# The even w_gate chunks of an attention and SwiGLU kernel: two tiles become one, with the four row blocks of a chunk in another place and another order

## The chip, the core and the metric

The kernel runs on one core of a Trainium2 chip. The metric is the device time of one execution in microseconds (us); the time before is the median of three runs.

## The reference, cut to what matters

Batch 8, 8 heads, 576 positions, 64 elements per head, all in float32. The attention output is laid out as 4608 rows of 512 and goes through a gated feed-forward layer.

```python
scores = (1.0 / np.sqrt(64)) * np.matmul(q, k.transpose(0, 1, 3, 2))
scores = np.where(block_i >= block_j, scores, -1e9)      # blocks of 64 positions
attn = softmax(scores)                                   # rows
x = np.matmul(attn, v).transpose(0, 2, 1, 3).reshape(4608, 512)
g = x @ w_gate                                           # 512 x 1536
silu = g * (1.0 / (1.0 + np.exp(-g)))
out = (silu * (x @ w_val)) @ w_out                       # 1536 x 512
```

## The kernel before

Attention runs by batch and by pairs of heads: TensorE makes scores, VectorE and GpSimd the maxima, ScalarE the exponentials, TensorE the products with v. The feed-forward layer runs on 18 tiles of 256 rows of x. Every float32 operand of its products is split into a high and a low part (`float32r`), and a product is the sum of three matmuls: high by high, high by low, low by high.

In `feed_forward`, each of the 18 tiles walks through the 12 column chunks of 128 of w_gate and w_val two at a time. For one such pair, `up(i, 0)` multiplies x with w_gate's even chunk and then with its odd chunk, and `up(i, 1)` does the same with w_val. A chunk has four blocks of 128 rows (d = 0 to 3, the four blocks of x^T in `xhl`), each with three matmuls of 256 columns: 12 matmuls a chunk, with the weights as the stationary operand (lines 1109 to 1111). The down products with w_out have the activations `hhl` as the stationary operand and 512 columns (lines 1201 to 1203).

All of w_gate and w_val stays in SBUF. `g_odd0`, `g_odd1` (high and low part of the odd chunks), `v_all0`, `v_all1` (w_val) and `g_even0`, `g_even1` are tiles of the pool `const`, placed one after the other. A tile `gap` of 64 bytes stands ahead of `g_even0`. In the built program `g_odd` starts at bytes 1984 and 14272 of a partition and `v_all` at 26560 and 51136, which is 192 modulo 256; `g_even` starts at 75776 and 88064, which is 0 modulo 256. The steps between a tile's blocks and chunks are multiples of 512 bytes, so each block of 128 columns starts at the same byte modulo 256 as its tile.

`weight(i, kind)` brings a chunk from HBM, puts its two int32 words together (ScalarE and VectorE) and writes the high part with ScalarE and the low part with VectorE into the place that `w_at` names. For six chunks, w_out's parts wait in such a place too (`AWAY`), before that place gets its own weights.

The order of all engines comes from a planner in the kernel, `in_order()`. Each piece of work is a task with an engine, a cost and a rank, and each waits for named others. In tiles 0 to 3 (`j < FINE`) the up product of each d is a task of its own, which waits for that d's x; from tile 4 on, the 12 matmuls of a chunk are one task. The x of tile 0 comes from the heads in turn: d = 0 from heads 0 and 1, d = 3 from heads 6 and 7. Where the plan leaves TensorE idle for over 0.3 us, `keep_busy` writes small matmuls of a tile of ones (line 1418) into the order ahead of the next task. After the first 8 us of the plan it writes `int(FILL * t.gap / 0.107)` of them, with `FILL` 0.6. Nothing reads their output. A change of what a task waits for can so move every later task, on every engine.

Of the kernel before, what the change touches and what calls it, by code (L numbers as in the profile page):

```python
# [7 lines left out]
F32 = mybir.dt.float32  # L8
F32R = mybir.dt.float32r
# [9 lines left out]
def kernel(  # L19
# [17 lines left out]
    nc = tc.nc  # L37
# [3 lines left out]
    P = 128  # L41
# [5 lines left out]
    NDC = DM // P  # L47
    NFC = DFF // P
# [12 lines left out]
    FINE = 4  # L61
# [35 lines left out]
    const = ctx.enter_context(tc.tile_pool(name="const", bufs=1))  # L97
# [55 lines left out]
    def add(engine, cost, rank, fn, after=(), bufs=(), port=False, mode="", stage=""):  # L153


        t = Task(engine, cost, rank, fn, after, bufs, port, mode)
        for a in after:
            if a is not None:
                a.next.append(t)
                t.waits += 1  # L160
        for u in bufs:
            u.left += 1
        t.n, t.stage = len(tasks), stage
        tasks.append(t)
        return t


    def act_us(n, psum=False, more=0.0):
        return (0.05 if psum else 0.093) + n * 0.000833 + more

    def dve_us(n, one=False):
        return 0.07 + n * (0.00052 if one else 0.00104)

    def up_us(n):
        return n * 0.1134 + (0.012 if n < 3 * NDC else 0.0)
# [8 lines left out]
    def dma(rank, size, fn, after=(), bufs=(), n=1, engine="SP", packet=1024, late=0.0):  # L184

        t = add(engine, 0.5 * n, rank, fn, after, bufs)
        t.moves = size / packet * (6.0 + 0.0485 * packet) / 16e3
        t.late = 1.1 + late
        return t
# [12 lines left out]
    half_w, whole_w = [P, NDC, DFF // 2], [P, NDC, DFF]  # L202
    g_odd = [const.tile(half_w, F32R, name=f"g_odd{x}") for x in range(2)]
    v_all = [const.tile(whole_w, F32R, name=f"v_all{x}") for x in range(2)]
    const.tile([P, 16], F32, name="gap")
    g_even = [const.tile(half_w, F32R, name=f"g_even{x}") for x in range(2)]

    def w_at(which, x, i):

        if which:  # L210
            return v_all[x][:, :, i * P : (i + 1) * P]
        return (g_odd if i % 2 else g_even)[x][:, :, i // 2 * P : (i // 2 + 1) * P]

# [98 lines left out]
    for i in range(7):  # L314
        n = 2**i
# [594 lines left out]
    def words(ap):  # L910
        return ap.bitcast(I32) if wide else ap
# [11 lines left out]
    def weight(i, kind):  # L923

        R = PIECES[i][kind]
        raw = Buf("wo", "raw")
        away = AWAY.get(i) if kind == 2 else None
        wo = Buf("wo", "out") if kind == 2 and not away else None
        fs = slice(i * P, (i + 1) * P)

        parts = 1 if wo else NDC

        def part(j):  # L940
            if wo:
                return wo[0][:, j : j + 1]
            which, c = away or (kind, i)
            return w_at(which, j, c)

        def load():
            view = raw[0].rearrange("p (n m) -> p n m", n=NDC if kind < 2 else 1)
            if kind < 2:
                fs = slice(i * P * (1 + wide), (i + 1) * P * (1 + wide))
                src = words((w_gate, w_val)[kind])[:, fs].rearrange("(c p) f -> p c f", p=P)  # L950
            else:
                src = words(w_out)[i * P : (i + 1) * P, :].rearrange("p (n m) -> p n m", n=1)
            nc.sync.dma_start(out=view, in_=src)

        t = chain["w"] = dma(AHEAD.get((i, kind), R), 5e5, load, [chain["w"]], [raw], packet=1024 if kind < 2 else 4096)
        bufs = [raw, wo] if wo else [raw]

        def words_of(j):
            w = raw[0].rearrange("p (n t) -> p n t", t=1 + wide)[:, :, j]
            return w.rearrange("p (n m) -> p n m", n=parts)  # L960

        y = Buf("ob", "signs") if wide else None


        def signs():
            w = words_of(1).bitcast(F32)
            to = y[0].rearrange("p (n m) t -> p n m t", n=parts)[:, :, :, 1]
            nc.scalar.mul(to, w, 2.0**-60)

        def scaled():  # L970
            w = words_of(1).bitcast(F32)
            nc.scalar.mul(w, w, 2.0**-112)


        def fraction():
            s = y[0].rearrange("p m t -> p (m t)").bitcast(I32).rearrange("p (n m) -> p n m", n=parts)
            nc.vector.scalar_tensor_tensor(
                words_of(0), words_of(0), 29, s, ALU.logical_shift_right, ALU.bitwise_or
            )

        def exponent():
            nc.vector.scalar_tensor_tensor(
                words_of(0), words_of(1), 3, words_of(0), ALU.logical_shift_left, ALU.bitwise_or
            )

        def high():
            nc.scalar.copy(part(0), words_of(0).bitcast(F32))

        def low():
            nc.vector.tensor_tensor(  # L990
                part(1), words_of(0).bitcast(F32), part(0).bitcast(F32), ALU.subtract
            )

        if wide:
            t = add("ACT", act_us(DM, more=0.13), R, signs, [t], [raw, y])
            f = add("DVE", dve_us(DM), R, fraction, [t], [raw, y], True)
            t = add("ACT", act_us(DM, more=0.06), R, scaled, [t], [raw])
            t = add("DVE", dve_us(DM), R, exponent, [t, f], [raw], True)
        t = w_high[i, kind] = add("ACT", act_us(DM, more=0.04), R, high, [t], bufs)
        t = add("DVE", dve_us(DM), R, low, [t], bufs, True)  # L1000
        if kind == 2:
            w_kept[i] = t, wo, part

            def store():
                if wo:
                    nc.sync.dma_start(out=wo_d[i], in_=wo[0].bitcast(F32))
                    return
                for j in range(2):
                    nc.sync.dma_start(
                        out=wo_d[i][:, j].rearrange("p (n m) -> p n m", n=parts), in_=part(j).bitcast(F32)  # L1010
                    )

            t = dma(R, 5e5, store, [t], [wo] if wo else [], 2 if away else 1, packet=512 if away else 4096)
            if away:
                before_place.append((t, away))
        w_done[i, kind] = t
# [58 lines left out]
    def feed_forward(j, t0, w, xs):  # L1075
# [16 lines left out]
        def rank(i):  # L1092
            return (10.0 + (t0 + w * i / NFC) / S) if j > 1 else SIDE[j] + w * i / NFC / S

        def up(i, which, prev):

            ps = Buf("gv")
            ts = up_done[0]
            for y in range(2):

                for ds in [range(NDC)] if j >= FINE else [[d] for d in range(NDC)]:

                    def products(ds=ds, y=y):
                        hi, lo = (w_at(which, k, i + y) for k in range(2))
                        o = ps[0][:, y * w : (y + 1) * w]
                        for d in ds:
                            xhi, xlo = (xs[d][1][k] for k in range(2))
                            first, last = d == 0, d == NDC - 1
                            nc.tensor.matmul(o, lhsT=hi[:, d], rhs=xhi[:, 0:w], start=first, stop=False)  # L1109
                            nc.tensor.matmul(o, lhsT=hi[:, d], rhs=xlo[:, 0:w], start=False, stop=False)  # L1110
                            nc.tensor.matmul(o, lhsT=lo[:, d], rhs=xhi[:, 0:w], start=False, stop=last)  # L1111

                    ts = add(
                        "PE",
                        up_us(3 * len(ds)),
                        rank(i),
                        products,
                        [ts, *(xs[d][0] for d in ds), w_done[i + y, which]],
                        [ps, *(xs[d][1] for d in ds)],
                        stage="up",  # L1120
                    )
                    ts.prev = prev
                    prev = ts if j >= FINE else None
            chain["up"] = up_done[0] = ts
            return ps, ts

        for i in range(0, NFC, 2):
            t, hh = Buf("t"), Buf("hhl")
            soon, chain["soon"] = chain["soon"], chain["up"]
            pg, tg = up(i, 0, None)  # L1130
            if j < 2:
                soon = tg
# [6 lines left out]
            n = 2 * w  # L1139
# [29 lines left out]
            for y in range(2):  # L1169
                away = AWAY.get(i + y)  # L1170
                if j == 0 or j == 1 and i + y < BOTH:
                    wl, wo, w_part = w_kept[i + y]
                else:
                    wo, away = Buf("wo", "out"), None
# [42 lines left out]
        for m in range(nb):  # L1217

            halves = 2 if ends_alone and m == nb - 1 else 1
            for x in range(halves):  # L1220
                ob = Buf("t") if x else Buf("ob", "out")
                cols = slice(x * DM // halves, (x + 1) * DM // halves)
# [231 lines left out]
```

## Time and profile before

| | |
|---|---|
| median of three runs | 1167.11 us (1166.97 to 1167.42) |
| the profiled execution: its time, and the span in its profile | 1170.11 us, 1168.3 us |
| granted TensorE clock, mean | 0.997 |
| busy: TensorE, its weight loads, VectorE, ScalarE, GpSimd | 1153.5, 1038.0, 743.6, 619.6, 321.1 us |

In the profile, PE is TensorE's matmuls, PEld its weight loads, DVE VectorE, ACT ScalarE, POOL GpSimd and SP the engine that issues most DMAs. Lines such as L1109 are lines of the kernel before. The end of a matmul in the trace is modelled and reaches into the next one, so the distance from one matmul's start to the next one's start is what a matmul costs in a stream. One small matmul of line 1418 in the order stands as two matmuls in the trace.

### The profile page before, as it was taken

How to read it: one execution, taken by the hardware profiler on the slowest of the kernel's cores; microseconds unless marked ns; L12 is line 12 of the kernel's file. 1: busy time of each engine (PE TensorE's matmuls, PEld its weight loads, DVE VectorE, ACT ScalarE, POOL GpSimd, SP SyncE). 2: the span in 40 equal slices, each digit the busy share in tenths (PEclk: the TensorE clock that was granted, in tenths of full speed). 3: DMA queues.
4: the chain of work that ended last, by engine and by line, in shares of the span. 5: the costliest groups of instructions: out<-in, count | busy, mean ns of one | idle time of the engine just before them, and what ended most of it. 6: DMA issues, size and time to landing. Idle time of an engine off the chain costs nothing.

```text
span 1168.3 us, 22310 instructions
## 1 busy us (share of the span) xinstructions
PE 1153.5 (99%) x8744; PEld 1038.0 (89%) x8744; DVE 743.6 (64%) x1230; ACT 619.6 (53%) x1114; POOL 321.1 (27%) x141
## 2 busy tenths in 40 slices
PE   7999999999999999999999999999999999999998
PEld 6778788889899989898998989898998989999997
DVE  4998898877697857576774747576575643323222
ACT  5889776745675655473745555473655422212111
POOL 3213100153525263334133423333133420000000
PEclk8999999999999999999999999999999999999999
DMA  7857756766557466653756565663664445444352
GB/s 185 228 153 213 192 189 226 213 197 170 159 150 210 116 183 181 195 151 114 189 166 197 140 182 144 199 159 123 175 196 149 144 142 170 145 162 138 142 172 100
DMA packets 266986, 197.44 MB, mean 169 GB/s; under 512 B 195264, under 2 KB 231376, under 8 KB 266880
## 3 DMA queue, kind: packets, MB, share of 16 engines
q1 hardware_dynamic: 264304, 195.29, 57.3%
q8 instruction: 69, 1.13, 0.4%
q10 hardware_dynamic: 2576, 0.72, 0.3%
q14 instruction: 37, 0.30, 0.1%
HBM read 171.57 MB, written 24.38 MB: 168 GB/s over the span
## 4 chain that ended last, share of the span: by engine, by line
PE 91%; ACT 4%; DMA 2%; DVE 2%; issue 1%; POOL 0%; SPq 0%; POOLq 0%; ACTq 0%
PE gv L1109 17%; PE gv L1111 16%; PE gv L1110 16%; PE at L829 8%; PE po L1201 8%; PE po L1203 7%; PE po L1202 7%; PE at L578 6%; PE at L451 1%; ACT sc L469 1%; PE at L1201 1%; DMA wo<-in_moe_w_gate_dram 1%; PE at L1202 1%; PE at L1203 1%; PE at L662 1%
## 5 line engine op out<-in xcount | busy, mean ns | idle before, releaser
L723 POOL PARTITION_ALL_REDUCE mx<-mx x80 | 140.6, 1805 | 395.3 <-DVE mx L719 184.6
L1109 PE MATMUL gv<-xhl,v_all 128*128 128x256 f32 x864 | 241.2, 279 | 0.1
L880 POOL PARTITION_ALL_REDUCE mx<-mx x48 | 178.3, 3768 | 228.2 <-DVE mx L719 214.6
L1111 PE MATMUL gv<-xhl,v_all 128*128 128x256 f32 x864 | 239.1, 277 | 0.0
L1110 PE MATMUL gv<-xhl,v_all 128*128 128x256 f32 x864 | 239.0, 277 | 0.0
L1146 DVE SCALAR_TENSOR_TENSOR t<-t,gv 128x512 f32<-128x512 f32 x108 | 73.9, 684 | 164.4 <-ACT t L1143 163.8
L1109 PEld LDWEIGHTS gv<-xhl,v_all 128*128 128x128 f32 x864 | 162.1, 188 | 3.5 <-issue 1.6
L1110 PEld LDWEIGHTS gv<-xhl,v_all 128*128 128x128 f32 x864 | 162.2, 188 | 0.5
L1111 PEld LDWEIGHTS gv<-xhl,v_all 128*128 128x128 f32 x864 | 162.2, 188 | 0.0
L1156 ACT CAST hhl<-t 128x512 fp32r<-128x512 f32 x108 | 67.1, 622 | 165.0 <-PE po L1202 93.5
L1201 PE MATMUL po<-wo,hhl 128*128 128x512 f32 x372 | 147.5, 397 | 0.0
L1203 PE MATMUL po<-wo,hhl 128*128 128x512 f32 x372 | 145.2, 390 | 0.3 <-DVE hhl L1159 0.3
L1202 PE MATMUL po<-wo,hhl 128*128 128x512 f32 x372 | 145.5, 391 | 0.0
L1159 DVE TENSOR_TENSOR hhl<-t,hhl 128x512 fp32r<-128x512 f32 x108 | 82.2, 763 | 90.3 <-ACT hhl L1156 90.0
L747 DVE TENSOR_TENSOR sc<-sc,mx 128x640 f32<-128x640 f32 (+6 forms) x168 | 122.8, 772 | 16.2 <-POOL mx L723 16.0
L1143 ACT ACTIVATE t<-gv 128x512 f32<-128x512 f32 x108 | 64.6, 598 | 119.3 <-PE gv L1111 114.3
L1151 DVE SCALAR_TENSOR_TENSOR t<-t,gv 128x512 f32<-128x512 f32 x108 | 73.9, 684 | 81.6 <-PE gv L1111 80.8
L1109 PE MATMUL gv<-xhl,g_even 128*128 128x256 f32 x432 | 123.8, 286 | 0.0
L751 ACT ACTIVATE sc<-sc 128x1024 f32<-128x1024 f32 (+3 forms) x104 | 105.7, 1032 | 31.8 <-DVE sc L747 31.2
L1111 PE MATMUL gv<-xhl,g_even 128*128 128x256 f32 x432 | 122.1, 283 | 0.0
L1110 PE MATMUL gv<-xhl,g_even 128*128 128x256 f32 x432 | 122.1, 283 | 0.0
L1109 PE MATMUL gv<-xhl,g_odd 128*128 128x256 f32 x432 | 120.5, 279 | 0.0
(173 smaller groups left out, 2465.9 us busy)
## 6 DMA issues: line engine op xcount, KB each, us to landing
wo<-wo_d SPq DMA_DIRECT2D x200, 512.0 KB
out_dram<-ob SPq DMA_DIRECT2D x35, 256.0 KB
v<-in_v_dram SPq DMA_DIRECT2D x64, 128.0 KB
xt<-x_d SPq DMA_DIRECT2D x64, 128.0 KB
rt<-r_d SPq DMA_DIRECT2D x128, 64.0 KB
qk<-in_q_dram SPq DMA_DIRECT2D x112, 72.0 KB
qk<-in_k_dram SPq DMA_DIRECT2D x104, 72.0 KB
x_d<-xu SPq DMA_DIRECT2D x24, 288.0 KB
```

The lines of the kernel that those rows point to most:

```text
L723: nc.gpsimd.partition_all_reduce(m, m, channels=P, reduce_op=bass_isa.ReduceOp.max)
L747: nc.vector.tensor_tensor(piece(c), scores_of(c), m, ALU.subtract)
L751: nc.scalar.activation(x, x, AF.Exp)
L829: nc.tensor.matmul(ps[0][own(x), 1 - i if sums else i, q0 - s0 : s1 - s0], lhsT=ones if sums else vt[0][:, 2 * lane + c, own(x)], rhs=sc[0 ...
L880: nc.gpsimd.partition_all_reduce(m, m, channels=P, reduce_op=bass_isa.ReduceOp.add)
L1109: nc.tensor.matmul(o, lhsT=hi[:, d], rhs=xhi[:, 0:w], start=first, stop=False)
L1110: nc.tensor.matmul(o, lhsT=hi[:, d], rhs=xlo[:, 0:w], start=False, stop=False)
L1111: nc.tensor.matmul(o, lhsT=lo[:, d], rhs=xhi[:, 0:w], start=False, stop=last)
L1159: nc.vector.tensor_tensor(hh[1][:, 0:n], t[0][:, 0:n], hh[0][:, 0:n].bitcast(F32), ALU.subtract)
L1201: nc.tensor.matmul(po, lhsT=hi, rhs=whi, start=i + y == 0, stop=False)
L1202: nc.tensor.matmul(po, lhsT=hi, rhs=wlo, start=False, stop=False)
L1203: nc.tensor.matmul(po, lhsT=lo, rhs=whi, start=False, stop=i + y == NFC - 1)
```

## The change

`g_even0` and `g_even1` become one tile `g_even`, which starts at byte 75712 (192 modulo 256). Its first half holds rows 0 to 255 of w_gate (d = 0 and 1) of all even chunks, high and low part by turns. 64 bytes further on, at byte 88064 (0 modulo 256), its second half holds rows 256 to 511 (d = 2 and 3). `turns_of` has the products of an even chunk run through d = 2, 3, 0, 1 in place of 0, 1, 2, 3. All other tiles stay where they were.

```diff
-    const.tile([P, 16], F32, name="gap")
-    g_even = [const.tile(half_w, F32R, name=f"g_even{x}") for x in range(2)]
+    rows_half = NFC * NDC // 2 * P
+    g_even = const.tile([P, 2 * rows_half + 16], F32R, name="g_even")
...
-        return (g_odd if i % 2 else g_even)[x][:, :, i // 2 * P : (i // 2 + 1) * P]
+        if i % 2:
+            return g_odd[x][:, :, i // 2 * P : (i // 2 + 1) * P]
+        o = (i + x) * NDC // 2 * P
+        one = g_even[:, o : o + NDC // 2 * P]
+        part, cols = one.ap
+        return bass.AP(one.tensor, one.offset, [part, [rows_half + 16, 2], cols])
+
+    def rows_of_w(w, d):
+
+        n = NDC // w.shape[1]
+        return w[:, d // n, d % n * P : (d % n + 1) * P]
+
+    def turns_of(which, i):
+
+        return (*range(NDC // 2, NDC), *range(NDC // 2)) if not which and i % 2 == 0 else tuple(range(NDC))
...
-                for ds in [range(NDC)] if j >= FINE else [[d] for d in range(NDC)]:
+                every_d = turns_of(which, i + y)
+                for ds in [every_d] if j >= FINE else [[d] for d in every_d]:
...
-                            first, last = d == 0, d == NDC - 1
-                            nc.tensor.matmul(o, lhsT=hi[:, d], rhs=xhi[:, 0:w], start=first, stop=False)
+                            first, last = d == every_d[0], d == every_d[-1]
+                            nc.tensor.matmul(o, lhsT=rows_of_w(hi, d), rhs=xhi[:, 0:w], start=first, stop=False)
```

The change moves the order of the program. The first place is TensorE's order at the start, about 30 us into the trace of before, where tile 0's first even chunk begins. Before, its product of d = 0 (`xhl_0_87`, `xhl_1_88`) stands between the scores (line 451) of a later pair of heads, after seven fillers:

```order
L1418 MATMUL gv_0_183<-ones 64x64 x7
L1109 MATMUL gv_0_183<-xhl_0_87,g_even_73 128x256
L1110 MATMUL gv_0_183<-xhl_1_88,g_even_73 128x256
L1111 MATMUL gv_0_183<-xhl_0_87,g_even_74 128x256
L451 MATMUL at_0_161<-parts_0_81,parts_1_82 128x320 x2
L451 MATMUL at_0_161<-parts_0_81,parts_1_82 128x64 x2
L451 MATMUL at_0_213<-parts_0_81,parts_1_82 128x320 x2
L1418 MATMUL gv_0_189<-ones 64x64 x12
```

The same place in the changed program, where a line's number is 14 or 15 higher:

```order
L1433 MATMUL gv_0_181<-ones 64x64 x11
L465 MATMUL at_0_159<-parts_0_79,parts_1_80 128x320 x2
L465 MATMUL at_0_159<-parts_0_79,parts_1_80 128x64 x2
L465 MATMUL at_0_211<-parts_0_79,parts_1_80 128x320 x2
L1433 MATMUL gv_0_181<-ones 64x64 x13
```

The chunk now begins with d = 2 and waits for the x of heads 4 and 5; its products of d = 0 and 1 come 46 rows further on, and fillers stand in their place. From here on the two orders differ, on all engines, up to about 860 us.

The second place is TensorE's order about 159 us into the trace of before, where the softmax sums (`mx` by `ones`) and the products with v of a pair of heads follow on up products of w_val. Before:

```order
L1109 MATMUL gv_0_189<-xhl_0_91,v_all_70 128x256
L1110 MATMUL gv_0_189<-xhl_1_92,v_all_70 128x256
L1111 MATMUL gv_0_189<-xhl_0_91,v_all_71 128x256
L812 MATMUL at_0_161<-mx_0_296,ones 64x320 x2
L829 MATMUL at_0_161<-sc_0_358,v_0_77 64x320 x6
L829 MATMUL at_0_161<-sc_0_358,v_0_77 64x192 x2
L829 MATMUL at_0_161<-sc_0_358,v_0_77 64x64 x2
L1109 MATMUL gv_0_189<-xhl_0_93,v_all_70 128x256
```

After:

```order
L1124 MATMUL gv_0_181<-xhl_0_99,v_all_70 128x256
L1125 MATMUL gv_0_181<-xhl_1_100,v_all_70 128x256
L1126 MATMUL gv_0_181<-xhl_0_99,v_all_71 128x256
L1433 MATMUL at_0_159<-ones 64x64 x50
L826 MATMUL at_0_159<-mx_0_294,ones 64x320 x2
L843 MATMUL at_0_159<-sc_0_356,v_0_75 64x320 x6
L843 MATMUL at_0_159<-sc_0_356,v_0_75 64x192 x2
L843 MATMUL at_0_159<-sc_0_356,v_0_75 64x64 x2
L1433 MATMUL gv_0_187<-ones 64x64 x8
L465 MATMUL at_0_159<-parts_0_82,parts_1_83 128x320 x2
```

Fifty fillers stand ahead of the sums and eight behind the products with v. Ahead of the sums stand 45 up and 6 down matmuls fewer than before, and 14 more fillers than before in earlier rows. In the whole order the fillers of line 1418 go from 116 in 20 groups to 196 in 27 groups; every other kind of matmul keeps its number.

The third place is an even chunk of a late tile, where a chunk is one task. Its twelve matmuls keep their place in the order, between the down products ahead of them and the odd chunk behind them. Before:

```order
L1203 MATMUL po_0_262<-wo_0_2451,hhl_1_111 128x512
L1109 MATMUL gv_0_189<-xhl_0_95,g_even_73 128x256
L1110 MATMUL gv_0_189<-xhl_1_96,g_even_73 128x256
L1111 MATMUL gv_0_189<-xhl_0_95,g_even_74 128x256
L1109 MATMUL gv_0_189<-xhl_0_97,g_even_73 128x256
```

After:

```order
L1218 MATMUL po_0_260<-wo_0_2216,hhl_1_107 128x512
L1124 MATMUL gv_0_181<-xhl_0_97,g_even 128x256
L1125 MATMUL gv_0_181<-xhl_1_98,g_even 128x256
L1126 MATMUL gv_0_181<-xhl_0_97,g_even 128x256
L1124 MATMUL gv_0_181<-xhl_0_99,g_even 128x256
```

The four blocks of x are `xhl` 93 to 99 here (95 to 101 before): the chunk starts with its third.

More of the change, by code (lines that the diff above doesn't have):

```diff
@@ L936, in weight @@
         fs = slice(i * P, (i + 1) * P)
-        parts = 1 if wo else NDC
         def part(j):
@@ L944, in part @@
             return w_at(which, j, c)
+        parts = 1 if wo else part(0).shape[1]
         def load():
@@ L1099, in up, with products @@
             for y in range(2):
-                for ds in [range(NDC)] if j >= FINE else [[d] for d in range(NDC)]:
-                    def products(ds=ds, y=y):
+                every_d = turns_of(which, i + y)
+                for ds in [every_d] if j >= FINE else [[d] for d in every_d]:
+                    def products(ds=ds, y=y, every_d=every_d):
                         hi, lo = (w_at(which, k, i + y) for k in range(2))
@@ L1107, in products @@
                             xhi, xlo = (xs[d][1][k] for k in range(2))
-                            first, last = d == 0, d == NDC - 1
-                            nc.tensor.matmul(o, lhsT=hi[:, d], rhs=xhi[:, 0:w], start=first, stop=False)
-                            nc.tensor.matmul(o, lhsT=hi[:, d], rhs=xlo[:, 0:w], start=False, stop=False)
-                            nc.tensor.matmul(o, lhsT=lo[:, d], rhs=xhi[:, 0:w], start=False, stop=last)
+                            first, last = d == every_d[0], d == every_d[-1]
+                            nc.tensor.matmul(o, lhsT=rows_of_w(hi, d), rhs=xhi[:, 0:w], start=first, stop=False)
+                            nc.tensor.matmul(o, lhsT=rows_of_w(hi, d), rhs=xlo[:, 0:w], start=False, stop=False)
+                            nc.tensor.matmul(o, lhsT=rows_of_w(lo, d), rhs=xhi[:, 0:w], start=False, stop=last)
                     ts = add(
```

## The prediction

> **What bounds the kernel now.** I read the page first: busy time, the tenths, the chain that ended last. Then TensorE's busy time by stage.
>
> ```profile
> PE 1153.5 (99%) x8744; PEld 1038.0 (89%) x8744; DVE 743.6 (64%) x1230; ACT 619.6 (53%) x1114; POOL 321.1 (27%) x141
> PE   7999999999999999999999999999999999999998
> PE 91%; ACT 4%; DMA 2%; DVE 2%; issue 1%; POOL 0%; SPq 0%; POOLq 0%; ACTq 0%
> 0.00:20.00 20.00, 13.73 (x133) 11.80 (x134) 7.26 (x27) 8.97 (x20) 6.78 (x16) 0.97 0.69 167
> 20.00:180.00 160.00, 155.56 (x1286) 124.36 (x1287) 140.38 (x263) 132.46 (x247) 35.75 (x29) 0.98 0.70 195
> 180.00:1060.00 880.00, 879.57 (x6585) 804.37 (x6584) 568.56 (x898) 459.28 (x817) 278.56 (x96) 1.00 0.58 168
> 1060.00:1168.30 108.30, 104.68 (x745) 97.49 (x743) 27.36 (x42) 18.84 (x33) 0.00 (x0) 1.00 0.40 138
> ```
>
> In the four stage rows the numbers after the width are busy us of PE, PEld, DVE, ACT and POOL. TensorE is the bound: from 180 us on it is idle for 0.43 us of 880 up to 1060. From 20 to 180 us it is idle for 4.44 us, and there VectorE (140.38 of 160) and ScalarE (132.46) are nearly as full. So every nanosecond that TensorE's own list grows or shrinks moves the end by as much, whether it is work or filler. Only 4.44 + 0.43 = 4.9 us of idle time between 20 and 1060 us could swallow an addition.
>
> **The alignment, the change's first part.** Groups by line and tile show that the tile matters:
>
> ```profile
> L1109 PE MATMUL gv<-xhl,g_even 128*128 128x256 f32 x432 | 123.8, 286 | 0.0
> L1110 PE MATMUL gv<-xhl,g_even 128*128 128x256 f32 x432 | 122.1, 283 | 0.0
> L1109 PE MATMUL gv<-xhl,g_odd 128*128 128x256 f32 x432 | 120.5, 279 | 0.0
> L1110 PE MATMUL gv<-xhl,g_odd 128*128 128x256 f32 x432 | 119.4, 276 | 0.0
> ```
>
> The last number ahead of the second bar is the mean in ns: the same product takes 7 ns more on g_even. The timeline (start, duration) shows it as a distance of starts:
>
> ```profile
> 519.69 0.28 PE L1109 MATMUL gv<-xhl,g_even 128*128 128x256 f32 x1
> 519.80 0.28 PE L1110 MATMUL gv<-xhl,g_even 128*128 128x256 f32 x1
> 519.92 0.28 PE L1111 MATMUL gv<-xhl,g_even 128*128 128x256 f32 x1
> 520.04 0.28 PE L1109 MATMUL gv<-xhl,g_even 128*128 128x256 f32 x1
> ...
> 521.00 0.28 PE L1111 MATMUL gv<-xhl,g_even 128*128 128x256 f32 x1
> 521.12 0.28 PE L1109 MATMUL gv<-xhl,g_odd 128*128 128x256 f32 x1
> ...
> 522.48 0.28 PE L1109 MATMUL gv<-xhl,v_all 128*128 128x256 f32 x1
> ```
>
> From 520.04 to 521.00 eight g_even matmuls cost 0.12 us each; the odd chunk's twelve take 522.48 - 521.12 = 1.36 us, 113.3 ns each. Each g_even matmul that comes to run like g_odd saves 6.7 ns. The change moves six of a chunk's twelve to g_odd's place modulo 256, and puts the six that stay ahead of them. In this stream the slow step is steady from the third matmul on, and the step to g_odd is fast at once. So I take it that after six slow ones the other six are fast: 6 x 6.7 = 40 ns a chunk. Tiles 4 to 17 have 14 x 6 = 84 chunks: 3.4 us. Tiles 0 to 3 have 24 chunks, whose 144 moved matmuls are mixed with other work, and there g_odd's place isn't always fast:
>
> ```profile
> 275.39 0.39 PE L1203 MATMUL po<-wo,hhl 128*128 128x512 f32 x1
> 275.62 0.28 PE L1109 MATMUL gv<-xhl,v_all 128*128 128x256 f32 x1
> 278.45 0.28 PE L1109 MATMUL gv<-xhl,g_even 128*128 128x256 f32 x1
> 279.89 0.28 PE L1109 MATMUL gv<-xhl,g_odd 128*128 128x256 f32 x1
> 281.30 0.28 PE L1109 MATMUL gv<-xhl,v_all 128*128 128x256 f32 x1
> ```
>
> Here, right after down products (0.23 us from start to start), 24 v_all matmuls take 2.83 us (117.9 each), and after 12 g_even at 120 the g_odd ones still take 117.5. A stream can thus stay in a middle rhythm. The 144 save 2 to 6.7 ns each, 0.3 to 1.0 us. Sum of this part: 3.7 to 4.4, I take -4.0 us.
>
> A rule of the Trainium skill speaks against it. "SBUF — State Buffer", section "Who interferes with whom", says that TensorE never waits on anyone at its SBUF ports, and "TensorE: Matmul & The Clock Gate", section "Step-by-step: what each phase is for", says that loading the next weights takes no read bandwidth from the running matmul. By these a shift of 64 bytes gives 0 us. The 7 ns between g_even and g_odd contradict them as far as the tiles' places are its cause, which one profile can't prove.
>
> **The order, the change's second part.** Starting with d = 2 makes tile 0's first chunk wait for heads 4 and 5, and the plan of every engine changes behind it. The order shows 80 more fillers, in 7 more groups: 160 matmuls in the trace. Their price, from the timeline (with the row that follows each group):
>
> ```profile
> 33.17 1.61 PE L1418 MATMUL gv<-ones 128*64 128x64 f32 x24
> 35.05 0.55 PE L425 MATMUL at<-ident,qk 96*128 96x96 f32 x4 [0.27 <-ACT sc L483]
> 46.80 1.15 PE L1418 MATMUL gv<-ones 128*64 128x64 f32 x16
> 48.20 0.71 PE L425 MATMUL po<-ident,qk 96*128 96x96 f32 x6 [0.26 <-ACT sc L483]
> 48.85 0.68 PE L1418 MATMUL gv<-ones 128*64 128x64 f32 x8
> 49.46 0.39 PE L1109 MATMUL gv<-xhl,g_even 128*128 128x256 f32 x1
> ```
>
> 24 fillers against 8 are busy 1.61 - 0.68 = 0.93 us longer: 58 ns each. The group of 8 holds the next work off by 49.46 - 48.85 = 0.61 us, 0.14 us over 8 x 58 ns. So 160 fillers and 7 groups cost at least 160 x 0.058 + 7 x 0.14 = 10.3 us, since TensorE runs its list in order. They cost more where the work behind them isn't ready: the group of 16 at 46.80 delays the next work by 1.40 us, 88 ns each; at that rate 160 make 14.0 us. These are the ends, 10.3 and 14.0.
>
> Which end? Most of it is the group of fifty ahead of the softmax sums. In the trace of before:
>
> ```profile
> 157.12 0.82 DVE L719 TENSOR_TENSOR mx<-mx,sc 128x640 f32<-128x640 f32 x1
> 159.34 0.76 PE L812 MATMUL at<-mx,ones 128*64 128x320 f32 x4
> ```
>
> VectorE ends the last addition of these sums at 157.94, 1.4 us before TensorE uses them. After the change TensorE has 45 up (0.116 us) and 6 down matmuls (0.23 us) less ahead of it, 6.6 us, and 14 more filler pairs, 1.6 us. It comes 5.0 us earlier. If nearly full VectorE keeps its time, TensorE would wait 5.0 - 1.4 = 3.6 us; fifty pairs take 100 x 0.058 + 0.14 = 5.9 us. The fillers then cover the wait, and the low end holds. I take 10.3 + 0.5 for waits elsewhere.
>
> What the fillers give back: behind them VectorE and ScalarE are 2.3 us ahead (5.9 - 3.6), so that later waits of that stage shrink, such as this one:
>
> ```profile
> 175.05 0.76 PE L812 MATMUL at<-mx,ones 128*64 128x320 f32 x4 [0.72 <-issue]
> ```
>
> That is -0.7; the bounds are 0 and the 4.9 us of idle time, and I stay near 0 because the new order will have waits of its own. The deferred products themselves cost nothing new: they are run later, in a stage without idle time, and this is why the fillers are paid in full.
>
> At nothing: the writes of the weight parts keep their size (512 elements a partition), and ScalarE and VectorE do them beside TensorE; without that cover each would cost its duration, as much as before. The four DMAs from g_even's place to wo_d move the same bytes in longer pieces. The products themselves keep their number.
>
> **The sum.** -4.0 + 10.3 + 0.5 - 0.7 = +6.1 us. The profiled execution took 1170.11 us, its span and 1.8 us around it, and becomes 1176.2; it is 3.0 above the median of the runs. On the median, 1167.11 + 6.1 = 1173.2 us. About 0.2%, 2.3 us, is what a measurement can tell from no change.
>
> **Rivals.**
> - *The fillers are swallowed; no slower than before.* The one mechanism is that VectorE's lead takes away the later idle time: all 4.9 us, and the end is +6.1 + 0.7 - 4.9 = +1.9, 1169.0 us. It decides from 4.5 us of idle time removed. For it: fillers stand where TensorE would only run ahead of VectorE. Against it: a part of that idle time lies before the fifty, at 33 to 50 us as shown above. Chance 0.13.
> - *TensorE waits beyond the fillers and its clock falls.* Price: 14.0 in place of 10.8, and part of the stage at half clock. This trace has the case:
>
> ```profile
> 15.54 0.56 PE L1418 MATMUL gv<-ones 128*64 128x64 f32 x6
> 19.10 0.87 PE L425 MATMUL at<-ident,qk 96*128 96x96 f32 x4 [3.00 <-DMA qk<-in_q_dram]
> 19.91 1.86 PE L1418 MATMUL gv<-ones 128*64 128x64 f32 x15
> ```
>
> After 3.00 us of idle time fifteen fillers are busy 1.86 us, over 110 ns each. Two us of such work more makes 1173.2 + 3.2 + 2 = 1178.4 us. It needs VectorE over 2.3 us later than I take it. Chance 0.13.
> - *The address has no part in it,* and g_even is slow because it follows other work: 0 in place of -4.0, 1177.2 us. Against it: v_all after down products is slow by 4.6 ns, not 6.7, with g_odd's place modulo 256. This is also the skill's rule of ports that never wait. Chance 0.08.
> - *The six don't settle the rhythm.* The middle rhythm (117.9) then holds for the moved six, the odd chunk and w_val's 24: 36 x 4.6 - 6 x 2.1 = 0.15 us a chunk pair. In all 108: +16, and +4.0 lost: 1193. In a third of them, 1180. For it: the rows from 275.62 on. Against it: the steady 120 ns from the third matmul in the late tiles. Chance 0.06.
>
> **How the numbers follow.** The forecast, 1170 to 1177 (terms at their ends: -4.4 to -3.7, 10.3 to 14, idle 0 to -3), has 0.57; with the four rivals 0.40; the rest, a gain that I can't derive, 0.03. The range 1169.2 to 1179.0 holds the forecast, most of the second and third rivals and a part of the first: 0.8. Slower by over 0.2% (above 1169.4): the forecast and the last three, 0.84, and 0.02 of the first. Faster: 0.03. The same: 0.11.
>
> **What would show it.** Line 1418's new line has 392 matmuls, about 100 of them near 150 us in one group, and TensorE's idle time from 20 to 180 us stays at 3 to 5 us. In late tiles an even chunk takes 1.39 us from its first start to g_odd's, with a step from 120 to 113 ns at its seventh matmul, and g_odd stays at 1.36. From 180 us on TensorE is without idle time and reaches the same product some 9 us later, and the end 6 us later. I am wrong if the fifty come when TensorE would have waited before, too; if the late chunks still take 1.43; or if the new order of DMAs leaves TensorE waiting for weights behind 180 us.

## The result and the profile after

The changed kernel took 1181.67 us (median of 4, 1179.02 to 1182.12) beside 1167.26 us for the kernel before: a ratio of 1.0115, 95% interval 1.0102 to 1.0128, 12 to 15 us slower. The prediction was 1173.2 us, with a range up to 1179.0: right in sign, but the 6.1 us forecast are less than half of what was lost. The profiled executions took 1181.78 and 1170.11 us; their spans, 1180.0 and 1168.3 us, differ by 11.7.

First the page's busy time, then TensorE's stages, with the columns of the prediction's stage rows:

```profile
PE 1165.0 (99%) x8904; PEld 1048.2 (89%) x8904; DVE 742.9 (63%) x1230; ACT 619.5 (52%) x1114; POOL 318.8 (27%) x141
```

```profile
0.00:20.00 20.00, 16.99 (x136) 14.31 (x137) 7.37 (x27) 10.00 (x21) 6.77 (x16) 0.81 0.74 183
20.00:180.00 160.00, 154.06 (x1368) 124.19 (x1367) 137.35 (x260) 129.53 (x242) 35.22 (x26) 0.99 0.69 190
180.00:1060.00 880.00, 877.57 (x6579) 801.47 (x6578) 567.37 (x895) 459.08 (x817) 276.79 (x99) 1.00 0.58 167
```

TensorE executes 160 matmuls more, as forecast, and its busy share stays at 99%. But it is idle for 5.94 us from 20 to 180 us (4.44 before) and for 2.43 us from 180 to 1060 (0.43 before), where I had forecast 3 to 5, and none.

The groups and the timeline of a late tile show the first part of the change at work:

```profile
L1124 PE MATMUL gv<-xhl,g_even 128*128 128x256 f32 x432 | 122.8, 284 | 0.3 <-DVE t L1161 0.3
L1125 PE MATMUL gv<-xhl,g_even 128*128 128x256 f32 x432 | 120.7, 279 | 0.0
```

```profile
524.59 0.28 PE L1124 MATMUL gv<-xhl,g_even 128*128 128x256 f32 x1
...
525.30 0.28 PE L1124 MATMUL gv<-xhl,g_even 128*128 128x256 f32 x1
...
525.64 0.28 PE L1124 MATMUL gv<-xhl,g_even 128*128 128x256 f32 x1
...
525.98 0.28 PE L1124 MATMUL gv<-xhl,g_odd 128*128 128x256 f32 x1
...
527.34 0.28 PE L1124 MATMUL gv<-xhl,v_all 128*128 128x256 f32 x1
```

The chunk takes 525.98 - 524.59 = 1.39 us, and the odd one 1.36, both as forecast. Its first six take 0.71 us, and from the seventh (525.30) to the odd chunk six take 0.68, the last three of them 0.34: 113 ns each.

The second part shows ahead of the softmax sums (a bracket is idle time and what ended it):

```profile
153.97 6.04 PE L1433 MATMUL at<-ones 128*64 128x64 f32 x100
161.18 0.76 PE L826 MATMUL at<-mx,ones 128*64 128x320 f32 x4 [1.16 <-DVE mx L733]
...
163.79 1.10 PE L1433 MATMUL gv<-ones 128*64 128x64 f32 x16
165.48 1.13 PE L465 MATMUL at<-parts,parts 64*128 64x320 f32 x8 [0.59 <-ACT sr L899]
166.54 0.39 PE L1124 MATMUL gv<-xhl,g_even 128*128 128x256 f32 x1
```

TensorE reached the sums' place at 153.97; forecast was 159.34 less 5.0, or 154.3. VectorE had been taken to end the sums at 157.94, as before, and behind the fillers nothing was to wait. TensorE waited for VectorE until 161.18 instead, and ran no product of the feed-forward until 166.54: fillers, a wait, 2.6 us of attention, fillers, a wait, attention again. What VectorE did there:

```profile
155.31 0.69 DVE L991 SCALAR_TENSOR_TENSOR wo<-wo,ob 128x512 int32<-128x512 int32 x1
...
156.84 0.69 DVE L996 SCALAR_TENSOR_TENSOR wo<-wo 128x512 int32<-128x512 int32 x1
157.45 0.69 DVE L1174 TENSOR_TENSOR hhl<-t,hhl 128x512 fp32r<-128x512 f32 x1
159.08 0.69 DVE L991 SCALAR_TENSOR_TENSOR wo<-wo,ob 128x512 int32<-128x512 int32 x1 [0.95 <-ACT ob L982]
159.69 1.34 DVE L733 TENSOR_TENSOR mx<-mx,sc 128x640 f32<-128x640 f32 x1
```

The last addition (L733) ends at 161.03, 3.1 us later than 157.94, behind instructions that put weights together (L991, L996) or split the activations (L1174), one of which waits for ScalarE.

To see the whole, I added the distances from each TensorE matmul's start to the next one's, over the whole trace, by kind, with idle time apart (us; the middle kernel is the first experiment below):

| | before | late turns only | after |
|---|---|---|---|
| fillers | 20.05 | 20.10 | 30.34 |
| idle | 10.16 | 7.36 | 10.41 |
| g_even products | 158.01 | 154.70 | 154.54 |
| g_odd and v_all products | 449.42 | 450.52 | 450.86 |
| down products | 300.32 | 300.55 | 300.58 |
| attention | 225.34 | 226.90 | 228.26 |
| sum | 1163.30 | 1160.13 | 1174.99 |

The fillers grew by 10.3 us, the number predicted to a tenth, and g_even's products shrank by 3.5. The first 30 us differ between the profile before (5.4 us of idle time, clock 0.97 up to 20 us) and the other two (2.7 and 2.8 us, clock 0.81); at the same matmul about 30 us in, late turns only is 1.1 us ahead of before. So the middle column is the fair base for idle time. From it to the last the sum grows by 14.9 us: fillers 10.2, idle time 3.05, attention 1.4, all else 0.2.

### The profile page after: what moved, and what is told of

It reads as the page before. It is cut to its first block, busy times and chain, and to the rows that moved or that the text cites. A ratio compares the mean times of both kernels' runs of the same rounds, so it can differ in the third digit from the quotient of the medians.

```text
span 1180.0 us, 22626 instructions
## 1 busy us (share of the span) xinstructions
PE 1165.0 (99%) x8904; PEld 1048.2 (89%) x8904; DVE 742.9 (63%) x1230; ACT 619.5 (52%) x1114; POOL 318.8 (27%) x141
## 4 chain that ended last, share of the span: by engine, by line
PE 75%; DVE 1%; ACT 0%; issue 0%; DVEq 0%
PE gv L1124 14%; PE gv L1126 14%; PE gv L1125 14%; PE po L1216 7%; PE po L1218 7%; PE po L1217 7%; PE at L592 6%; PE at L843 5%; PE at L1217 0%; PE at L1216 0%; PE at L1218 0%; ACT sc L602 0%; DVE mx L733 0%; DVE parts L560 0%; ACT ob L1243 0%
## 5 line engine op out<-in xcount | busy, mean ns | idle before, releaser
L1174 DVE TENSOR_TENSOR hhl<-t,hhl 128x512 fp32r<-128x512 f32 x108 | 81.5, 754 | 105.1 <-ACT hhl L1171 104.8
L1124 PE MATMUL gv<-xhl,g_even 128*128 128x256 f32 x432 | 122.8, 284 | 0.3 <-DVE t L1161 0.3
L1126 PE MATMUL gv<-xhl,g_even 128*128 128x256 f32 x432 | 120.8, 280 | 0.0
L1125 PE MATMUL gv<-xhl,g_even 128*128 128x256 f32 x432 | 120.7, 279 | 0.0
```

Source lines behind the costliest of these rows:

```text
L1124: nc.tensor.matmul(o, lhsT=rows_of_w(hi, d), rhs=xhi[:, 0:w], start=first, stop=False)
L1125: nc.tensor.matmul(o, lhsT=rows_of_w(hi, d), rhs=xlo[:, 0:w], start=False, stop=False)
L1126: nc.tensor.matmul(o, lhsT=rows_of_w(lo, d), rhs=xhi[:, 0:w], start=False, stop=last)
L1174: nc.vector.tensor_tensor(hh[1][:, 0:n], t[0][:, 0:n], hh[0][:, 0:n].bitcast(F32), ALU.subtract)
```

## Experiments

Ratios are to the kernel before, run on the same chip (its median there was 1168.3 to 1168.9 us).

| kernel | median us | ratio, 95% interval |
|---|---|---|
| late turns only | 1166.53 | 0.9982 (0.9973 to 0.9991) |
| halves swapped, old order | 1166.16 | 0.9982 (0.9973 to 0.9991) |
| new order, old places | 1186.47 | 1.0154 (1.0140 to 1.0167) |
| gap behind g_even | 1178.45 | 1.0080 (1.0065 to 1.0095) |
| four at 0 modulo 256 | 1177.73 | 1.0077 (1.0063 to 1.0091) |
| after without the fifty | 1185.17 | 1.0142 (1.0126 to 1.0158) |
| the same, sums first on VectorE | 1183.33 | 1.0123 (1.0109 to 1.0137) |
| fifty in the old plan | 1170.94 | 1.0024 (1.0013 to 1.0035) |
| tile 0 turned | 1173.30 | 1.0041 (1.0026 to 1.0056) |
| tiles 1 to 3 turned | 1172.56 | 1.0033 (1.0019 to 1.0046) |
| chunk 6 early | 1175.53 | 1.0061 (1.0046 to 1.0076) |
| chunk 6 at rank 40 | 1177.18 | 1.0083 (1.0066 to 1.0101) |

My theory was that the new plan is the whole loss and the places a gain; the rival, that the places or the joint tile have no part, or cost. I start with the two parts taken apart.

**Late turns only.**

```diff
-                every_d = turns_of(which, i + y)
+                every_d = turns_of(which, i + y) if j >= FINE else tuple(range(NDC))
```

> The changed layout of g_even, but the turns 2, 3, 0, 1 only from tile 4 on; tiles 0 to 3 take 0, 1, 2, 3. The planner then puts every instruction where the kernel before has it, with the same fillers. Theory (the new plan is the whole loss, the places are a real gain): the late even chunks save 14 x 6 x 40 ns = 3.4 us, tiles 0 to 3 between 0 and 1 us, so 1163.3 us (1162.5 to 1164.2) against 1167.2 for the kernel before. Rival (the joint tile or its places cost in themselves, and the plan only a part): no gain or slower, 1167 to 1172 us.

**Halves swapped.** The base of the access pattern moves to the second block and the step turns negative:

```diff
-        return bass.AP(one.tensor, one.offset, [part, [rows_half + 16, 2], cols])
+        return bass.AP(one.tensor, one.offset + rows_half + 16, [part, [-(rows_half + 16), 2], cols])
...
-                every_d = turns_of(which, i + y)
+                every_d = tuple(range(NDC))
```

> The order 0, 1, 2, 3 everywhere, so the plan of the kernel before, and the halves of g_even's chunks swapped: rows 0 to 255, which come first, at 0 modulo 256, and rows 256 to 511 at 192 modulo 256. Theory (place and turn are all that the step of 113 ns needs, the new plan is the whole loss): 84 late even chunks save 40 ns each, 3.4 us, and the 24 early ones 0 to 1 us: 1163.3 us (1162.5 to 1164.2). Rival (the six slow ones don't settle the rhythm where a stream comes out of down products in tiles 0 to 3): up to 1 us lost there, 1164 to 1165 us. Second rival (places that count run modulo the half's own step, not the address): 1167.2 us.

**New order, old places.** w_at and g_even as in the kernel before, turns_of as in the changed kernel.

> The turns 2, 3, 0, 1 everywhere, so the changed kernel's plan and its fillers, but g_even's tiles and places as in the kernel before (all rows at 0 modulo 256). Theory (the order alone is the loss): the even chunks fall back to 120 ns a matmul, so the changed kernel's 1181.7 us plus 3.4 to 4.4, 1185 to 1186 us. Rival (the address has no part in the step of 113 ns): the same 1181.7 us.

Both kernels with the old plan are faster than the kernel before, by 0.18%, 1.1 to 3.2 us, and both beat the changed kernel; the runs don't tell the two apart. Without the new places the changed kernel is slower by another 0.39%, 4.6 us. About 2.2 us of it lie in the steps of the up products (g_even's 3.8 more, the others 1.6 less), and from 30 us on another 1.7 us are idle time, most of it the wait for the sums:

```profile
163.07 1.33 PE L821 MATMUL at<-mx,ones 128*64 128x320 f32 x4 [2.47 <-DVE mx L728]
```

That wait is 2.47 us in place of 1.16, and the clock column reads 0.50 from 163 to 166 us. The theory holds in sign on both sides: the places gain, and the order loses 1.33%, 15.5 us (changed kernel against late turns only). The size of the gain fell short of the 3.4 us and more that I expected. The table says where: from tile 4 on g_even's products take 120.82 us before and 117.61 with late turns, 3.2 less (38 ns a chunk, forecast 40), but g_odd's and v_all's behind them take 0.27 more; in tiles 0 to 3 nothing is gained on balance (gains of 0.1 and 0.6 us in g_even's products are lost in the others). "SBUF — State Buffer" of the Trainium skill, section "Who interferes with whom", by which TensorE waits on nobody at its ports, would have the places give 0; the measured interval excludes 0.

**Gap behind g_even.** Does a weight's place alone set its step, or the stream?

```diff
-    const.tile([P, 16], F32, name="gap")
     g_even = [const.tile(half_w, F32R, name=f"g_even{x}") for x in range(2)]
+    const.tile([P, 16], F32, name="gap")
```

> The kernel before with the 64-byte gap behind g_even in place of ahead of it: all of g_even comes to 192 modulo 256, like the moved half of the changed kernel; same plan, same order of products, other tiles unmoved. Theory (a slow first half is needed to settle the rhythm): every stream that comes out of down products then runs its 48 matmuls at about 117.9 ns, 14 x 6 pairs of chunks x (48 x 117.9 - 12 x 120 - 36 x 113.3) ns = 12 us more in the late tiles, so about 1180 us against 1168. Rival (the place of each weight alone sets its step): all of g_even at 113.3 ns saves 14 x 6 x 12 x 6.7 ns = 6.8 us in the late tiles, 1161 us.

It is 0.80% slower, 9.4 us; in the late tiles its up products take 11.3 us more, where the theory had 12. Timeline of a late tile, and the groups of g_odd between 360 and 1000 us, first of this kernel, then of the kernel before:

```profile
542.28 0.39 PE L1203 MATMUL po<-wo,hhl 128*128 128x512 f32 x1
542.50 0.28 PE L1109 MATMUL gv<-xhl,g_even 128*128 128x256 f32 x1
...
543.92 0.28 PE L1109 MATMUL gv<-xhl,g_odd 128*128 128x256 f32 x1
...
545.33 0.28 PE L1109 MATMUL gv<-xhl,v_all 128*128 128x256 f32 x1
```

```profile
L1109 PE MATMUL gv<-xhl,g_odd 128*128 128x256 f32 x252 | 70.3, 279 | 0.0
```

```profile
L1109 PE MATMUL gv<-xhl,g_odd 128*128 128x256 f32 x256 | 70.7, 276 | 0.0
```

g_odd, which nobody moved, now takes 545.33 - 543.92 = 1.41 us a chunk (117.5 ns a matmul) in place of 1.36: the stream stays in the middle rhythm that it entered with. The rival by place alone (1161 us) is out.

**Four at 0 modulo 256.** How much is needed to settle? The low parts of rows 0 to 255 move to the fast places too:

```diff
-        o = (i + x) * NDC // 2 * P
+        o = i // 2 * NDC // 2 * P
+        if x:
+            return g_even[:, rows_half // 2 + 2 * o :][:, : NDC * P].rearrange("p (n m) -> p n m", n=2)
         one = g_even[:, o : o + NDC // 2 * P]
         part, cols = one.ap
-        return bass.AP(one.tensor, one.offset + rows_half + 16, [part, [-(rows_half + 16), 2], cols])
+        far = 3 * rows_half // 2 + 16
+        return bass.AP(one.tensor, one.offset + far, [part, [-far, 2], cols])
```

> The kernel with swapped halves, but only the high parts of rows 0 to 255 stay at 0 modulo 256; the low parts of these rows come to 64 modulo 128 as well, so that a chunk of twelve has four slow products (first, second, fourth, fifth) in place of six in a row; same plan as before. Theory (any few slow ones ahead settle the rhythm): two more of twelve at 113.3 ns, 84 x 2 x 6.7 ns = 1.1 us less than with six, 1165 us. Rival (the settling needs the slow ones in an unbroken row, or more than two): the late streams fall back to 117.9 ns as with the gap behind, about 1177 us.

```profile
540.93 0.28 PE L1127 MATMUL gv<-xhl,g_even 128*128 128x256 f32 x1
...
542.35 0.28 PE L1127 MATMUL gv<-xhl,g_odd 128*128 128x256 f32 x1
...
543.76 0.28 PE L1127 MATMUL gv<-xhl,v_all 128*128 128x256 f32 x1
```

Four products at the slow place, broken by one at a fast place, don't settle the stream: 1.41 us a chunk again, and 11 us lost against six in a row. Whether it is the number or the break was not tried.

**After without the fifty.** Now the order's part. The condition is on the count of that one group:

```diff
-        for _ in range(int(t.gap / 0.25 if t.at < 8.0 else FILL * t.gap / 0.107)):
+        count = int(t.gap / 0.25 if t.at < 8.0 else FILL * t.gap / 0.107)
+        for _ in range(0 if count == 50 else count):
```

> The changed kernel without the one group of fifty fillers near 150 us; nothing else differs. Theory (VectorE is later than the prediction took it, so the fifty stand where TensorE would wait anyway): the wait for the softmax sums, 1.16 us in the changed kernel's trace, grows to about 7 us, and the time stays at 1181 to 1182 us, or a few us above if the clock falls to half behind the wait. Rival (TensorE's list sets the end there, so that fillers are paid in full, as the prediction took them): 5.9 us less minus the part that turns into a wait, 1176 to 1179 us.

```profile
162.18 1.33 PE L826 MATMUL at<-mx,ones 128*64 128x320 f32 x4 [8.07 <-DVE mx L733]
```

The four us behind it, by engine and clock:

```profile
162.00:166.00 4.00, 3.82 (x16) 1.96 (x18) 4.00 (x8) 2.36 (x3) 0.00 (x0) 0.50 0.00 0
```

The fillers' 6.3 us turn into idle time, 8.07 us in place of 1.16, and the clock column reads 0.50 behind it (1.00 in the changed kernel): 1185.17 us, about 3 us slower (1.0142 against 1.0115; the two intervals just overlap). So the fifty cost nothing there; they cover a wait of some 7 us and keep the clock up. "TensorE: Matmul & The Clock Gate" of the Trainium skill, section "What's actually happening", has the clock halve after at least one idle window of about 3.4 us; the half clock behind 8.07 us agrees with it. The half clock behind 2.47 us above, and behind 1.77 us in the run with chunk 6 early below, comes after less idle time than the page names.

**The same, sums first on VectorE.** Is it VectorE's order? The two last additions (tasks 404 and 405) move behind 403:

```diff
     order = in_order()
+    early = [t for t in order if t.n in (404, 405)]
+    order = [t for t in order if t.n not in (404, 405)]
+    at = 1 + next(x for x, t in enumerate(order) if t.n == 403)
+    order[at:at] = early
```

> The changed kernel without the group of fifty, and with VectorE's two last additions of the softmax sums that TensorE then waits for moved ahead of ten other instructions of VectorE's list, directly behind the addition before them (they were 7 instructions of weight splitting and of the gate's product later); nothing else differs. Theory (TensorE's wait of 8.07 us there is the order of VectorE's list): the sums are ready near 154 us, where TensorE comes, the wait all but vanishes, and 1185.2 becomes 1177 to 1179 us, below the changed kernel's 1181.7. Rival (VectorE as a whole is behind, and what it puts off makes TensorE wait at the next place): the wait moves on, and the time stays at 1182 to 1186 us.

TensorE and, of the same kernel, ScalarE:

```profile
153.65 0.76 PE L826 MATMUL at<-mx,ones 128*64 128x320 f32 x4 [0.39 <-DVE mx L733]
...
165.52 2.08 PE L465 MATMUL at<-parts,parts 64*128 64x320 f32 x8 [8.16 <-ACT sr L899]
```

```profile
159.06 0.78 ACT L982 ACTIVATE ob<-wo 128x512 f16<-128x512 f32 x1 [2.29 <-DMA wo<-in_moe_w_gate_dram]
...
162.48 0.66 ACT L1001 CAST g_odd<-wo 128x512 fp32r<-128x512 f32 x1 [1.95 <-DVE wo L996]
```

The rival holds: the sums come at 153.65, and the same 8 us stand at the next place, behind ScalarE's list. My theory of VectorE's order alone fell. Behind the sums and the products with v TensorE has nothing to run up to 165 us, whichever engine the wait is put down to. I call this stretch, from 154 to 165 us, the hole.

**Fifty in the old plan.** The swapped kernel with fifty fillers where the sums are ready:

```diff
             if joined:
+                sums_seen.append(a)
+                if len(sums_seen) == 6:
+                    for _ in range(50):
+                        nc.tensor.matmul(ps[0][0:D, 0, 0:D], lhsT=ones, rhs=ones, start=True, stop=True)
                 sum_all()
```

> The kernel with swapped halves (the plan of the kernel before) with a group of fifty fillers ahead of the softmax sums that TensorE forms at 158 us, where VectorE has them ready; nothing else differs. Theory (fillers are paid in full where the work behind them is ready, and nothing comes back): 1166.2 + 5.9 = 1172 us. Rival (the lead that VectorE and ScalarE win behind them takes away later waits, as the prediction took it, 0.7 us and up to 3): 1169 to 1171.4 us.

It costs 0.42% over the swapped kernel, 3.3 to 6.5 us; the spans differ by 5.7. The steps of the fillers grow by 5.3 us, and the idle time falls by 0.34 us only. Fillers ahead of ready work are paid nearly in full. The median, 1170.94, lies where the rival had it, but the interval holds 5.9 us as well as 5.2: whether 0.7 us or nothing comes back is not told apart.

**Tile 0 turned, tiles 1 to 3 turned.** The condition on the turns becomes `j == 0 or j >= FINE`, or `j > 0`.

> The changed kernel with the turns 2, 3, 0, 1 in tile 0 and from tile 4 on; tiles 1 to 3 take 0, 1, 2, 3. The planner then places 32 more fillers than before (64 matmuls in the trace, six more groups), none of fifty. Theory (the late start of tile 0's products is the loss, and it shows at the fifty only because tile 1 adds to it): 64 x 0.058 + 6 x 0.14 = 4.6 us for fillers, and about 1 us of waits, on the 1166.5 us of the kernel with late turns alone: 1171 to 1173 us. Rival (tile 0 alone displaces the 6.6 us of products ahead of the sums, with or without fillers): 1177 to 1182 us.

> The changed kernel with tile 0 in the order 0, 1, 2, 3 and the turns 2, 3, 0, 1 in tiles 1 to 3 and from tile 4 on. The planner places 32 more fillers than before, none of fifty. Theory (tile 0's start is the main part of the loss): 32 fillers, 64 x 0.058 + 3 x 0.14 = 4.1 us, on 1166.5: 1170 to 1172 us. Rival (tile 1's turn is the main part): 1175 to 1182 us.

They lose 0.59% and 0.51% against late turns alone, 6.9 and 6.0 us, just above what was expected for fillers (4.6 and 4.1 us) and waits, 4.5 to 6.5 and 3.5 to 5.5. Neither has the hole: TensorE is busy for all of 150 to 170 us in both. Each part costs its fillers and some 2 us more, neither is the main part, and the hole needs both.

**Chunk 6.** What, then, is TensorE out of? I matched the writes of weights by VectorE with the planner's list, and compared when each of the 36 pieces was done, in the changed kernel and with late turns only. All but three are within 7 us of each other. The one farthest off is the low part of w_gate's chunk 6. Its row before, after, and with its rank changed:

```profile
121.32 0.69 DVE L990 TENSOR_TENSOR g_even<-wo,g_even 128x512 fp32r<-128x512 f32 x1 [1.08 <-ACT g_even L987]
```

```profile
165.03 0.68 DVE L1004 TENSOR_TENSOR g_even<-wo,g_even 128x512 fp32r<-128x512 f32 x1
```

```profile
118.19 0.70 DVE L1004 TENSOR_TENSOR g_even<-wo,g_even 128x512 fp32r<-128x512 f32 x1
```

It comes 44 us late, and TensorE's first product of the feed-forward after the hole (166.54 above) is one on that chunk. In the planner's table it has the last rank of all 36 pieces, 60.2941: the planner gives it to VectorE when nothing else is ready. In the old plan that was at 121 us; in the new one not before 165. With tile 0 alone turned it is done at 138.6 us, with tiles 1 to 3 at 122.1, and neither has the hole. w_out's chunk 7 is 25 us late, too (169.3 us), but with tile 0 alone turned it is 16 us late (160.7) and there is no hole. The test is one number:

```diff
     PIECES = [
...
-        (60.2941, 42.2325, 2.1654),
+        (-10.0, 42.2325, 2.1654),
```

> The changed kernel with one number of the planner's table changed: the rank of w_gate's chunk 6 (its load and its splitting on ScalarE and VectorE) is -10.0 in place of 60.2941. In the changed kernel's trace VectorE writes that chunk's low part at 165.7 us, in the kernel before at 122.0; with the new rank it stands 17th among the 36 weight pieces in place of 25th, and the planner places 26 more fillers than the kernel before, not 80, and no group of fifty. Theory (chunk 6 comes 44 us late, so TensorE has no product ready at 154 to 165 us, whatever stands there): the loss at that place, some 8 us, goes; 52 x 0.058 + 4 x 0.14 = 3.6 us of fillers and 1 to 3 us of waits stay on the 1166.5 us of the kernel with late turns alone: 1171 to 1174 us. Rival (the late chunk only goes along with the loss, and the late start of tile 0's products causes it whatever comes first): 1178 to 1182 us.

> As the run before, with a smaller step: the rank of w_gate's chunk 6 is 40.0 in place of 60.2941. The piece stands 18th of 36, and the planner places 41 more fillers than the kernel before, none of fifty. Theory (the late chunk is the loss at 154 to 165 us): 82 x 0.058 + 5 x 0.14 = 5.5 us of fillers and 1 to 3 us of waits on 1166.5 us: 1173 to 1175 us. Rival (as above): 1178 to 1182 us.

The stage from 150 to 170 us, of the changed kernel, of chunk 6 early, and of late turns only:

```profile
150.00:170.00 20.00, 18.25 (x211) 16.43 (x211) 18.29 (x31) 13.88 (x24) 3.78 (x2) 1.00 0.37 115
```

```profile
150.00:170.00 20.00, 20.00 (x161) 16.86 (x159) 18.32 (x32) 15.70 (x28) 2.77 (x2) 1.00 0.48 148
```

```profile
150.00:170.00 20.00, 20.00 (x146) 16.68 (x145) 17.55 (x32) 14.92 (x26) 2.47 (x2) 1.00 0.56 172
```

The changed kernel's 18.25 us hold 7.1 us of fillers, so that with 1.75 us idle it loses 8.9 us; with chunk 6 early the idle time is gone, and fillers take 0.7 us (0.56 and 1.4 us with rank 40). So the hole goes when chunk 6 comes in time, at two ranks. Each rank also moves the rest of the plan, and no other piece's rank was changed for comparison. Of the hole's 8 us 0.54% came through to the end, 6.3 us, and with rank 40 0.32%, 3.7 us: both runs lie between the theory's times and the rival's.

The new plans lose elsewhere. With chunk 6 early 9.2 us remain against late turns only. In the traces they are 3.7 us of fillers and 2.9 us of idle time, as the theory had them, and 2.6 us of slower steps, which it didn't have. Some 1.7 us of these lie in one place:

```profile
285.16 0.39 PE L1124 MATMUL gv<-xhl,g_even 128*128 128x256 f32 x1 [1.77 <-DVE t L1161]
284.00:290.00 6.00, 4.84 (x28) 4.84 (x29) 4.46 (x7) 1.56 (x3) 2.04 (x1) 0.72 0.12 47
```

TensorE waits 1.77 us for VectorE, and the clock column reads 0.72 in these 6 us (0.50 from 286 to 289), worth 6 x 0.28 = 1.7 us. Which part of the new plan brings these later waits was not tried.

## Why the prediction was wrong, point by point

- *The alignment, -4.0.* Right in mechanism, too large: -2.1 us (1.1 to 3.2). That six at the slow place leave the other six fast held in the late tiles, at 38 ns a chunk; the 0.3 to 1.0 us for tiles 0 to 3 did not come. Its third and fourth rivals are settled: the address has a part, and six products at 0 modulo 256 right behind down products do settle the rhythm, but a stream without them loses 9.4 us, by the mechanism of the fourth rival.
- *The fillers, 10.3.* The number was met, 10.24. The reason given for it, that fillers are paid in full "since TensorE runs its list in order", holds in the old plan, but fifty of the eighty stand in a hole and cost nothing there.
- *"If nearly full VectorE keeps its time, TensorE would wait 5.0 - 1.4 = 3.6 us."* This step failed. TensorE came when it was said to come, but VectorE ended the sums 3.1 us late, and without the fifty TensorE waited 8.07 us there, not 3.6. The fifty covered that wait but for 1.16 us, and the lead of 2.3 us behind them never came. The second rival, which decides from those 2.3 us, was the nearest, at 1178.4 us, though the clock stayed up at that place.
- The number of fillers had said so. By the kernel's formula fifty stand for 50 x 0.107 / 0.6 = 8.9 us of idle time in the plan, and 8.9 us is what the stage lost. All eighty stand for 14.3 us, where the order lost 15.5. It is no more than a first mark: with chunk 6 early, 26 more fillers stand for 4.6 us, and 9.2 were lost.
- *"The deferred products themselves cost nothing new."* This failed with it, and is the deeper one: products were deferred because the weights of chunk 6 were 44 us late, and TensorE's 6.6 us less of work ahead of the sums was the sign of a hole, not a lead to be won. With the chunk in time the loss fell by 6.3 us, and by 3.7 at rank 40.
- *"What the fillers give back", -0.7, and +0.5 for waits elsewhere.* Idle time grew by 3.05 us where -0.2 was the sum of the two: 1.75 us of it at the hole, 1.3 between 170 and 300 us. The steps of attention and of the products grew by 1.6, which the sum had at nothing. With 1.9 of the alignment this makes 6.7 of the 7 to 8 us that the forecast was short.
- *"The profiled execution is 3.0 above the median."* Only the spread of the runs: the kernel before took from 1166.7 to 1171.6 us beside the experiments.

## What to carry to other kernels

Where a planner places fillers, read their number as its forecast of idle time, and ask which input is late: compare the time at which each weight piece, tile or transfer becomes ready before and after, ahead of counting what the fillers cost. Where a change of order and a change of place come together, price them apart and, if the place can be had without the order (here by swapping two blocks), try them apart. A piece of the last rank that just fits one plan can be pushed out by tens of us when others shift by a few.

## What the runs showed of the hardware

- The step of fp32r products of 256 columns depends on where their weights start, and on the stream's past. At 0 modulo 256 bytes it is 120 ns. At 192 modulo 256, the only other place that was tried, it is 113.3 ns behind six or twelve products at 0 modulo 256 that came right behind down products, and 117.5 to 118 where the stream enters from down products without them, for all 48 products of it. Four of the first five at 0 modulo 256 were not enough, and neither were twelve behind 24 products of w_val in the kernel before (117.5 ns at 279.89 us). What in TensorE remembers this was not found.
- Fillers of 64 columns ahead of a wait of 7 us cost nothing and save about 3 us: without them the wait of 8.07 us is followed by half clock.
- Waits of 1.77 us (chunk 6 early, at 285 us) and 2.47 us (new order, old places, at 163 us) were followed by half clock; waits of 1.16 us (changed kernel, at 161 us) and 1.66 us (chunk 6 early, at 206 us) were not.
